# Another order and other engines for all operations of a fused attention and gated convolution kernel

## The chip, the cores and the metric

One core of a Trainium2 chip runs the whole program. The metric is device time in microseconds (us) of one launch. Five engines work side by side, each through its own list of instructions in order: TensorE (PE: matrix products, with weight loads shown as PEld), VectorE (DVE), ScalarE (ACT), GpSimd (POOL) and SyncE (SP, which issues the DMA transfers). An engine goes on only when the semaphores that its next instruction waits for have been set.

## The reference

Attention with a window and a few global keys for 4 batches x 8 heads x 768 queries x 64 elements, and then a gated convolution layer on its result. In the run `n_global` is 8 and `n_local` is 96.

```python
scores = scale * q @ k^T                      # per batch and head
is_global = pos[None, :] < n_global           # the first 8 keys
is_local = (rel >= 0) & (rel < n_local)       # the last 96 keys up to the query
dist = where(is_global & ~is_local, n_local, abs(rel))
scores = where(is_global | is_local, scores - slope[h] * dist, -1e9)
a = softmax(scores)                           # the sum gets 1e-9 added
x = a @ v                                     # heads side by side: (4, 768, 512)
gate = sigmoid(causal_conv(x, conv_w, 5 taps))    # for every channel apart
out = (gate * (x @ w_val)) @ w_out
```

The weights `w_val`, `w_out` and `conv_w` arrive as 64-bit floating point numbers, q, k and v in 32 bits; the result has 32 bits.

## The kernel before

The work is cut into 32 groups `g`: 4 batches x 2 halves of 384 queries x 4 pairs of heads. A group has three steps of 128 queries, 96 steps `s` in all. What a group goes through, with the name that the order table has for it, the line where its instruction is issued, and the engine:

- `L`, `LV`: SP loads the keys and queries `kq` and the values `va` of a group.
- `S` (line 598, PE): scores of the three steps, only for the keys that the window or the global keys can reach: at most 168 columns for each of the two heads.
- `AM` (line 606, DVE): adds the bias `bias` and takes the row minimum (`mins`) in one pass; two for each step.
- `EX` (line 616, ACT): exponential with row sum `sm`. `RG` (line 623, DVE or POOL): the guard 1e-9. `RC` (line 626, DVE): the reciprocal `rs`. `NM` (line 631, DVE or POOL): the normalisation of `p`, two for each step.
- `PT` (line 642, PE): transpositions into `pt`. `EV` (lines 298 and 300, ACT or DVE): copy of `pt` to `a`. `PV` (lines 662 and 668, PE): products with the values into `x`, for two groups together.
- `XS`, `XH`, `XL` (lines 298, 300 and 738): `x` copied to `xs` and split into a high and a low part, since an exact 32-bit product is made of three products of such parts. `CV` (lines 746 to 750): five filter taps into `gate`, the first of them on any of three engines, the others on DVE. `HI`: the four columns before a half.
- `SG` (line 779, ACT): tanh for the gate. `VM` (line 786, PE): product with `w_val`, four times four pieces of three products for each of the 8 phases (batch and half). `GM` (line 793, DVE): gate times value. `GH`, `GL` (lines 298, 300 and 800): its split.
- `OM` (line 809, PE): product with `w_out` into `o`. `OE` (lines 821 and 823): copy to `ob`. `ST` (line 828, SP): store.

Beside it run the weights, eight blocks of 128 rows or columns. `WL` loads one. `WA` (ACT) and `WZ` (line 484, POOL or DVE: the sign) read its upper halves, then DVE makes `h` (`W2`, line 494), the rounded `y` (`W3`, line 497) and the low part `r` (`W4`, line 500). `WH` copies the high part, `WS` (lines 525 to 527, PE) adds up in three products what is left into `wsum`, and `WP` copies that to the low half of the weights. `F` are filler products of PE on constants at the start (line 400), four at each of three places, and a table `FILL` names steps with further fillers before a transposition (line 637).

At the end stands a decision. If the numbers of global and local keys, or the scores, leave the range that the windows cover, a general path computes everything again after the fast one. `FA` (line 880, DVE) takes the maximum of all row minima, `FB` (line 884, PE) transposes it into `rmt`, and `FC` (lines 890 to 896, DVE) makes an integer `flag` from it in seven small instructions. Behind the last planned operation every engine reads `flag` (line 907) and branches on it (line 908). In the run the general path is not taken. The instructions of line 1119 close the program.

What sets the order: every operation is put into a plan with its kind, its engine and the operations and buffers that it needs. A table `SLOTS` has, for each kind, one number for each of its operations; the plan is sorted by it and issued in that order, and each engine receives its instructions in it. A table `ENGINES` has a letter for each operation of a kind that may run on several engines (V is DVE, S is ACT, G is POOL). Buffers are rings: an operation that reuses one waits for the readers of the old contents.

```python
e = NAMES[ENGINES[kind][n]] if kind in ENGINES else engines[0]
self.ops.append((SLOTS[kind][n], e, fn, list(deps)))
...
return [(fn, e) for _, e, fn, _ in sorted(self.ops, key=lambda op: op[0])]
...
plan.add(("FA",), (DVE,), row_mins, [("AM", s, j) for s in range(NSTEP) for j in range(2)])
plan.add(("FB",), (PE,), row_mins_t, [("FA",)] + plan.ring("pt", PT_B, ("FB",), [("FC",)]))
plan.add(("FC",), (DVE,), decide, [("FB",)])
```

Of the kernel before, what the change touches and what calls it, by code (L numbers as in the profile page):

```python
# [24 lines left out]
        2, 5, 7, 10, 30, 93, 98, 185, 233, 238, 250, 297, 338, 426, 480, 530, 594, 635, 679, 753, 845, 873, 937,  # L25
        972, 1030, 1084, 1133, 1169, 1236, 1464, 1472, 1479,
# [3 lines left out]
        19, 36, 87, 142, 191, 197, 202, 256, 275, 308, 361, 482, 485, 487, 588, 689, 718, 849, 854, 869, 1144, 1157,  # L30
        1160, 1163, 1231, 1239, 1262, 1469, 1475, 1484, 1620, 1625,
    ),
    "WARM": (0,),
    "F": (108, 27, 54),
    "IOTA": (1,),
    "UNITS": (15,),
    "CNT": (6,),
    "DIST": (9, 11),
    "BIAS": (12, 22, 13, 23, 20, 41, 18, 25, 24, 45, 26, 29, 28, 33, 37, 21),
    "WL": (4, 8, 77, 133, 175, 228, 302, 378),  # L40
    "WA": (39, 79, 139, 195, 231, 318, 394, 446),
    "WZ": (43, 106, 154, 200, 243, 328, 416, 476),
    "W2": (48, 110, 158, 211, 248, 344, 420, 483),
    "W3": (52, 117, 165, 216, 271, 354, 425, 488),
    "W4": (71, 128, 170, 220, 284, 372, 430, 497),
    "WH": (80, 127, 161, 217, 266, 355, 423, 490),
    "CWL": (14,),
    "CWA": (102,),
    "CW": (121,),
    "S": (  # L50
        17, 49, 72, 114, 166, 205, 245, 290, 333, 421, 471, 522, 587, 629, 672, 744, 796, 834, 933, 964, 1022, 1078,
        1124, 1158, 1217, 1293, 1355, 1411, 1467, 1532, 1576, 1662,
    ),
    "PV": (156, 260, 346, 453, 576, 701, 783, 922, 1007, 1142, 1250, 1341, 1453, 1567, 1699, 1751, 1778),
    "AM": (
        31, 32, 35, 38, 40, 42, 56, 58, 60, 64, 68, 69, 84, 89, 91, 94, 101, 104, 132, 135, 144, 149, 150, 160, 178,
        182, 188, 192, 194, 198, 227, 229, 232, 235, 237, 241, 257, 263, 265, 276, 278, 281, 306, 312, 316, 321,
        323, 326, 370, 377, 384, 386, 409, 414, 435, 437, 458, 461, 462, 466, 494, 495, 504, 508, 510, 513, 541,
        543, 555, 560, 573, 579, 598, 601, 605, 611, 620, 621, 638, 643, 649, 652, 654, 661, 697, 705, 712, 714,
        728, 737, 760, 767, 769, 779, 790, 793, 811, 818, 824, 826, 829, 830, 848, 863, 879, 882, 889, 891, 938,  # L60
        942, 945, 948, 950, 960, 979, 980, 993, 997, 1009, 1013, 1036, 1038, 1051, 1054, 1058, 1063, 1085, 1089,
        1096, 1102, 1116, 1118, 1135, 1136, 1141, 1145, 1147, 1154, 1170, 1178, 1185, 1198, 1200, 1206, 1225, 1232,
        1247, 1274, 1277, 1286, 1299, 1310, 1323, 1327, 1338, 1346, 1365, 1366, 1369, 1377, 1379, 1397, 1419, 1433,
        1438, 1441, 1443, 1446, 1476, 1486, 1501, 1515, 1520, 1522, 1540, 1541, 1543, 1546, 1549, 1556, 1582, 1594,
        1603, 1624, 1629, 1656, 1671, 1672, 1685, 1698, 1700, 1703,
    ),
    "EX": (
        34, 44, 47, 50, 53, 57, 61, 66, 70, 74, 85, 90, 95, 103, 109, 115, 122, 124, 136, 152, 157, 159, 164, 172,
        190, 209, 207, 212, 226, 236, 242, 246, 249, 262, 269, 289, 292, 294, 298, 307, 335, 343, 339, 349, 347,
        381, 373, 387, 397, 406, 400, 428, 419, 433, 450, 457, 481, 499, 496, 509, 518, 524, 547, 551, 561, 565,  # L70
        578, 582, 580, 583, 599, 619, 628, 631, 642, 657, 648, 650, 660, 665, 671, 677, 690, 711, 724, 729, 731,
        741, 756, 758, 765, 771, 778, 784, 809, 835, 839, 844, 855, 862, 870, 888, 892, 913, 898, 905, 908, 920,
        944, 947, 973, 1001, 975, 1004, 994, 1016, 1011, 1019, 1032, 1035, 1049, 1066, 1060, 1074, 1101, 1105, 1114,
        1120, 1122, 1128, 1125, 1149, 1139, 1151, 1184, 1203, 1191, 1207, 1199, 1248, 1224, 1243, 1230, 1237, 1265,
        1284, 1269, 1282, 1312, 1329, 1319, 1343, 1340, 1349, 1370, 1376, 1392, 1409, 1415, 1429, 1418, 1444, 1427,
        1440, 1448, 1471, 1452, 1454, 1480, 1491, 1519, 1528, 1524, 1536, 1547, 1563, 1569, 1571, 1589, 1593, 1616,
        1650, 1643, 1647, 1660, 1664, 1674, 1680, 1688, 1701, 1722, 1728,
    ),
    "RG": (
        46, 55, 76, 75, 81, 116, 123, 129, 140, 162, 167, 184, 215, 219, 244, 267, 287, 293, 301, 341, 351, 357,  # L80
        396, 402, 429, 445, 451, 464, 503, 517, 529, 564, 572, 597, 593, 627, 632, 663, 664, 670, 702, 740, 739,
        757, 780, 798, 788, 850, 876, 877, 899, 919, 924, 930, 996, 1008, 1010, 1021, 1025, 1040, 1072, 1079, 1111,
        1129, 1159, 1168, 1181, 1208, 1214, 1253, 1255, 1256, 1302, 1287, 1335, 1347, 1396, 1384, 1417, 1434, 1456,
        1455, 1478, 1489, 1497, 1533, 1564, 1575, 1584, 1610, 1661, 1665, 1705, 1708, 1737, 1730,
    ),
    "RC": (
        51, 63, 83, 88, 113, 120, 131, 145, 147, 169, 180, 189, 218, 225, 251, 270, 304, 310, 311, 350, 359, 371,
        401, 407, 434, 459, 465, 486, 506, 527, 536, 566, 596, 608, 609, 637, 641, 666, 693, 704, 707, 742, 747,
        766, 791, 800, 810, 856, 878, 903, 925, 928, 941, 946, 1012, 1015, 1020, 1041, 1046, 1070, 1087, 1095, 1127,
        1140, 1161, 1172, 1201, 1210, 1221, 1271, 1272, 1301, 1307, 1342, 1348, 1364, 1399, 1400, 1420, 1436, 1465,  # L90
        1481, 1492, 1500, 1534, 1545, 1574, 1579, 1602, 1644, 1670, 1689, 1721, 1723, 1738, 1742,
    ),
    "NM": (
        62, 59, 78, 67, 97, 99, 92, 96, 118, 125, 134, 138, 141, 148, 163, 176, 151, 181, 171, 193, 196, 186, 208,
        234, 239, 222, 230, 261, 255, 264, 280, 274, 309, 315, 327, 325, 319, 348, 362, 367, 385, 364, 375, 382,
        412, 405, 444, 441, 467, 472, 507, 470, 474, 516, 520, 519, 523, 511, 535, 563, 540, 567, 590, 577, 606,
        600, 612, 616, 634, 626, 640, 647, 659, 656, 673, 699, 713, 696, 710, 706, 719, 730, 746, 770, 763, 750,
        799, 773, 817, 814, 833, 802, 867, 838, 861, 871, 894, 881, 904, 912, 927, 935, 943, 939, 967, 970, 974,
        955, 1018, 1014, 1033, 1017, 1027, 1037, 1057, 1071, 1050, 1065, 1081, 1091, 1099, 1106, 1126, 1100, 1131,
        1138, 1153, 1174, 1164, 1173, 1188, 1183, 1215, 1216, 1242, 1219, 1228, 1222, 1275, 1280, 1295, 1279, 1305,  # L100
        1303, 1350, 1330, 1358, 1352, 1351, 1354, 1374, 1368, 1402, 1405, 1408, 1401, 1424, 1437, 1445, 1442, 1468,
        1490, 1502, 1485, 1523, 1512, 1527, 1535, 1565, 1562, 1553, 1548, 1605, 1597, 1634, 1596, 1628, 1622, 1666,
        1646, 1687, 1675, 1692, 1716, 1725, 1739, 1745, 1753, 1741, 1759, 1747, 1761,
    ),
    "PT": (
        65, 82, 105, 111, 126, 143, 153, 177, 201, 213, 214, 240, 253, 273, 282, 296, 330, 337, 358, 368, 392, 410,
        424, 448, 477, 512, 528, 544, 550, 568, 592, 603, 622, 633, 644, 655, 684, 716, 725, 751, 759, 775, 805,
        813, 822, 840, 880, 887, 900, 936, 949, 969, 989, 995, 1028, 1039, 1052, 1083, 1092, 1107, 1113, 1132, 1167,
        1179, 1196, 1209, 1223, 1261, 1267, 1297, 1304, 1311, 1361, 1372, 1380, 1393, 1423, 1430, 1447, 1474, 1506,
        1510, 1542, 1552, 1585, 1608, 1630, 1652, 1668, 1678, 1717, 1726, 1746, 1758, 1763, 1771,  # L110
    ),
    "EV": (
        73, 100, 112, 119, 137, 155, 174, 187, 206, 221, 223, 259, 272, 279, 303, 322, 334, 345, 369, 376, 408, 417,
        440, 452, 492, 526, 542, 558, 559, 574, 610, 613, 625, 639, 669, 700, 721, 738, 752, 764, 774, 781, 812,
        819, 825, 851, 885, 895, 911, 952, 968, 981, 992, 1000, 1045, 1069, 1080, 1088, 1104, 1110, 1117, 1150,
        1186, 1193, 1213, 1229, 1246, 1283, 1291, 1300, 1309, 1331, 1367, 1385, 1404, 1406, 1432, 1435, 1459, 1496,
        1509, 1517, 1560, 1566, 1609, 1614, 1651, 1655, 1677, 1682, 1724, 1729, 1749, 1764, 1769, 1774,
    ),
    "WS": (86, 130, 183, 224, 320, 379, 432, 498),
# [65 lines left out]
        1775, 1782, 1847, 1845, 1854,  # L185
    ),
    "FA": (1743,),
    "FB": (1777,),
    "FC": (1840,),
}  # L190
ENGINES = {
# [23 lines left out]
FILL = {}  # L215
# [907 lines left out]
```

## Time and profile before

| what | value |
| --- | --- |
| median of 3 runs | 267.73 us (267.15 to 268.79) |
| the profiled execution's own time | 267.06 us |
| its span in the trace | 265.3 us |
| mean granted TensorE clock | 0.998 of full speed |
| PE busy | 257.0 us, 97% |
| DVE busy | 227.5 us, 86% |
| ACT busy | 199.5 us, 75% |
| POOL busy | 96.6 us, 36% |
| HBM read and written | 29.46 MB and 6.29 MB, 135 GB/s over the span |

Times are counted from the span's start. Products of PE are pipelined, so a busy PE need not be doing its most; a product of 128x384 shows some 0.34 us and the next one starts after 0.18 us. Shares are means over stages that have different limits, so the stretches of the span are read apart. The engine names with a q at the end (PEldq, DVEq) are the parts of an engine that read registers, wait and branch.

### The profile page before, as it was taken

Reading aid. Unit: us, or ns where it says so; the run is one execution under the profiler, and the core shown is the slowest. Engines: PE = TensorE matmul, PEld = TensorE weight load, DVE = VectorE, ACT = ScalarE, POOL = GpSimd, SP = SyncE. Lnnn points to the kernel's source line nnn. Section 1 sums busy time; section 2 is a strip of 40 time slices with the busy share of each in tenths; the row PEclk is TensorE's granted clock in tenths of the full one; section 3 lists DMA queues with packets and bytes.
Section 4 is the critical chain, followed back from the end, with each engine's and each line's share of the span. In section 5 each row is a group of like instructions: output and inputs, shape, how many; then the busy total and the mean of one; then the engine's idle time right before and its main releaser. Section 6 shows DMA issues by size and latency. Waiting matters only on the chain.

```text
span 265.3 us, 8628 instructions
## 1 busy us (share of the span) xinstructions
PE 257.0 (97%) x3121; PEld 215.4 (81%) x3123; DVE 227.5 (86%) x920; ACT 199.5 (75%) x658; POOL 96.6 (36%) x211
## 2 busy tenths in 40 slices
PE   8699899999999999999999999999999999999994
PEld 3456697877899878998899878997898889878973
DVE  3998999889988999689898989799979898796930
ACT  3999999999989996977798586786978456546322
POOL 5676533462132659351131715131264410510020
PEclk9999999999999999999999999999999999999999
DMA  5996996326242730662112758100094042012003
GB/s 156 359 320 212 307 355 228 130 71 220 90 149 74 206 109 4 168 240 91 50 64 63 245 235 277 63 2 2 0 325 172 1 136 105 2 42 79 0 1 132
DMA packets 16305, 36.38 MB, mean 137 GB/s; under 512 B 1920, under 2 KB 4480, under 8 KB 16256
## 3 DMA queue, kind: packets, MB, share of 16 engines
q1 hardware_dynamic: 16256, 35.75, 40.2%
q8 instruction: 27, 0.44, 0.7%
q14 instruction: 22, 0.18, 0.2%
HBM read 29.46 MB, written 6.29 MB: 135 GB/s over the span
## 4 chain that ended last, share of the span: by engine, by line
PE 85%; DVE 6%; ACT 4%; issue 1%; DMA 1%; POOL 1%; ACTq 0%; POOLq 0%; DVEq 0%
PE o L809 25%; PE val L786 23%; PE pt L642 12%; PE s L598 9%; PE x L662 9%; PE x L668 4%; ACT p L616 2%; DVE gate L746 2%; PE wsum L525 1%; DMA counts_i<-in_counts 1%; DVE t L606 1%; POOL p L631 1%; ACT a L298 0%; DVE g L793 0%; ACT bias L464 0%
## 5 line engine op out<-in xcount | busy, mean ns | idle before, releaser
L616 ACT ACTIVATE p<-t,mins 128x168 f32<-128x168 f32 (+1 forms) x192 | 82.1, 430 | 15.5 <-PE pt L642 8.6
L631 POOL TENSOR_SCALAR p<-p,rs 128x168 f32<-128x168 f32 (+1 forms) x121 | 56.2, 475 | 82.5 <-DVE rs L626 59.8
L746 DVE SCALAR_TENSOR_TENSOR gate<-xs,cwt,gate 128x384 f32<-128x384 f32 x128 | 78.6, 631 | 0.7 <-ACT gate L748 0.4
L606 DVE CUSTOM_DVE_ANT_0 t<-s,bias 128x168 f32<-128x168 f32 (+1 forms) x192 | 55.7, 317 | 7.2 <-PE s L598 7.1
L642 PE MATMUL pt<-ident,p 128*128 128x128 f32 x272 | 47.3, 279 | 0.8 <-POOL p L631 0.5
L786 PE MATMUL val<-xh,wvh 128*128 128x384 f32 x128 | 47.5, 371 | 0.1
L786 PE MATMUL val<-xh,wvl 128*128 128x384 f32 x128 | 43.1, 337 | 0.0
L786 PE MATMUL val<-xl,wvh 128*128 128x384 f32 x128 | 43.1, 336 | 0.0
L809 PE MATMUL o<-woh,gh 128*128 128x512 f32 (+1 forms) x100 | 42.3, 423 | 0.0
L298 ACT COPY a<-pt 128x384 f32<-128x384 f32 (+1 forms) x81 | 36.3, 453 | 7.7 <-PE pt L642 7.6
L642 PEld LDWEIGHTS pt<-ident,p 128*128 128x128 f32 x272 | 33.0, 140 | 10.5 <-POOL p L631 1.6
L809 PE MATMUL o<-wol,gh 128*128 128x512 f32 (+1 forms) x100 | 38.6, 386 | 0.0
L809 PE MATMUL o<-woh,gl 128*128 128x512 f32 (+1 forms) x100 | 38.5, 385 | 0.0
L598 PEld LDWEIGHTS s<-kq 64*64 64x64 f32 x1088 | 30.1, 133 | 9.1 <-issue 5.6
L616 ACT ACTIVATION_READ_ACCUMULATOR p<-t,mins 128x1 f32 x192 | 37.3, 194 | 0.0
L598 PE MATMUL s<-kq 64*64 64x104 f32 (+3 forms) x1088 | 34.3, 262 | 2.1 <-DMA kq<-in_kq 1.7
L786 PEld LDWEIGHTS val<-xh,wvh 128*128 128x128 f32 x128 | 24.1, 188 | 0.9 <-DVE g L793 0.4
L821 ACT ACTIVATE ob<-o 128x512 f32<-128x512 f32 (+1 forms) x22 | 12.6, 577 | 16.2 <-PE o L809 16.2
L662 PE MATMUL x<-a,va 128*64 128x128 f32 x384 | 24.7, 277 | 0.0
L662 PEld LDWEIGHTS x<-a,va 128*64 128x64 f32 x384 | 20.6, 137 | 4.6 <-issue 3.8
L786 PEld LDWEIGHTS val<-xl,wvh 128*128 128x128 f32 x128 | 24.2, 189 | 0.0
L786 PEld LDWEIGHTS val<-xh,wvl 128*128 128x128 f32 x128 | 24.1, 188 | 0.0
(166 smaller groups left out, 396.6 us busy)
## 6 DMA issues: line engine op xcount, KB each, us to landing
kq<-in_kq SPq DMA_DIRECT2D x16, 444.0 KB, 4.6
va<-in_va SPq DMA_DIRECT2D x16, 384.0 KB, 6.6
out<-ob SPq DMA_DIRECT2D x24, 256.0 KB, 3.8
kq<-in_kq SPq DMA_DIRECT2D x15, 392.0 KB, 5.3
va<-in_va SPq DMA_DIRECT2D x16, 320.0 KB, 5.0
w<-in_wv SPq DMA_DIRECT2D x8, 256.0 KB, 4.5
w<-in_wo SPq DMA_DIRECT2D x3, 512.0 KB, 5.8
w<-in_wo SPq DMA_DIRECT2D x2, 256.0 KB, 3.6
```

What stands on the lines that cost most here:

```text
L298: nc.scalar.copy(dst, src)
L598: nc.tensor.matmul(s[rows, u : u + w], T["rq", g][r, k * P + half * QH : k * P + (half + 1) * QH], T["rk", g][r, c : c + w], start=True, s ...
L606: nc.vector.tensor_tensor_reduce(out=t[:, :n], in0=T["s", s // HB, s % HB, j][:, :n], in1=bias[:, h, :P] if n == P else bias[:, h, P:], op ...
L616: nc.scalar.activation(T["p", s][:, j, :n], T["t", s, j][:, :n], AF.Exp, bias=mins[:, s, j : j + 1], scale=-1.0, accum_out=T["sm", s][:, j ...
L631: engine(e).tensor_scalar(out=pr, in0=pr, scalar1=rs, scalar2=1.0, op0=ALU.mult, op1=ALU.mult)
L642: nc.tensor.transpose(pt[:, i * P : (i + 1) * P], pr[:, c : c + P], ident)
L662: nc.tensor.matmul(T["x", g][rows(i), c0 : c0 + P], T["near", g][:, k, j], T["a", HB * g + k][:, j * P : (j + 1) * P], start=k == 0, stop= ...
L668: nc.tensor.matmul(T["x", g][rows(i), c0 : c0 + QH], T["far", g][rows(j), k, h], T["a", HB * g + k][rows(j), 2 * P + h * QH : 2 * P + (h + ...
L746: nc.vector.scalar_tensor_tensor(out=gt, in0=src, scalar=w, in1=gt, op0=ALU.mult, op1=ALU.add)
L786: nc.tensor.matmul(T["val", ph, m], (wvh, wvh, wvl)[r][:, m, c * P : (c + 1) * P], (T["xh", g], T["xl", g], T["xh", g])[r], start=(c == 0 ...
L809: nc.tensor.matmul(T[key][:, cols], (T["gh", ph, c], T["gl", ph, c], T["gh", ph, c])[r][:, rows], (woh, woh, wol)[r][:, c, cols], start=(c ...
L821: nc.scalar.mul(dst, src, 0.5)
```

## The change

The two tables have other numbers and letters, and `FILL` names one step. No function is changed, and every operation of the plan is there as before. The numbers come from a longer search by annealing in which seven kinds of operations had other durations than in the search before. 45 of the 48 kinds in `SLOTS` have other numbers; a few rows are shown.

```diff
 SLOTS = {
     "L": (
-        2, 5, 7, 10, 30, 93, 98, 185, 233, 238, 250, 297, 338, 426, 480, 530, 594, 635, 679, 753, 845, 873, 937,
+        2, 5, 12, 19, 31, 92, 139, 146, 230, 316, 320, 399, 402, 412, 462, 517, 567, 734, 741, 802, 850, 991, 1016,
...
-    "F": (108, 27, 54),
+    "F": (55, 64, 28),
...
-    "FA": (1743,),
-    "FB": (1777,),
-    "FC": (1840,),
+    "FA": (1825,),
+    "FB": (1851,),
+    "FC": (1853,),
...
 ENGINES = {
-    "BIAS": "GGSSSGGGSSSSGGGV",
+    "BIAS": "SGSSSVSSVVSGGGGS",
-    "WZ": "GGGGGGGG",
+    "WZ": "GGVGGVGV",
...
     "NM": (
-        "GGVGVGGGGGGGGGVGGGGGGGVGGGGGGGGGGGVGGVVGGGGGGGGVGGGGVVVVVGVVGVVGGGGGVVGGVVGGGGGGGVGGGGGGGVGGGGGG"
-        "GGVVGGGGVVVVGGVVVVGVGVVVVGVGGGGVGGGGVVVVGGGGVVGVGVGGVGGGGVVVVGGGGGGGGVGVVVGGVVVVGGVVVVGVGVGVGVVV"
+        "VVGVGGGGVGGVGVGVVGGGVVVVVGGVVGVGVVVVVGGGVVVVGGGVGVGGGVGGVVGGGGGVVVGVVGVVGVGGGGVGVVVGVGVVVGGVVVVV"
+        "VGGVVVVGVVGVGVGGGGVVGVVGVVGVGGGGVVVVVGVVGGVVVVVVVVGVVVGVGVGVVGGVGVVVVGGVGGVVGGVGGVGVVVVVVVVVVVVV"
...
-FILL = {}
+FILL = {4: 1}
```

By the letters, the number of operations on each engine becomes: on DVE 772 instead of 712, on ACT 456 instead of 464, on POOL 143 instead of 195. Of the 192 normalisations `NM`, DVE has 112 instead of 71. SP issues the loads of the second weight block and of the taps ahead of the third `kq` instead of behind it, and the three sets of four fillers on PE stand one between the first and the second score group and two behind the second; before, one stood behind each of the first three score groups.

Three places are shown as rows of an engine's list. The names are those of the program's buffers, with their numbers; `[waits ...]` names the engines or DMA queues whose semaphore an instruction waits for.

The first is DVE around the low part of the fifth weight block, `('w', 4)_r`. Before:

```order
L497 TENSOR_SCALAR ('w', 4)_y_691<-('w', 4)_h_740 128x512
L606 ISA t_19_1_820,mins_85<-s_6_1_719,bias_78 128x168
L606 ISA mins_85 128x1
L606 ISA t_20_0_826,mins_85<-s_6_0_718,bias_78 128x168
L606 ISA mins_85 128x1
L606 ISA t_20_1_831,mins_85<-s_6_1_719,bias_78 128x168 [waits Activation_49]
L606 ISA mins_85 128x1
L500 SCALAR_TENSOR_TENSOR ('w', 4)_r_838<-w_4_560,('w', 4)_y_691 128x512 [waits DMAHW7_49,DMAHW6_49,DVE_49]
```

And in the change:

```order
L626 RECIPROCAL rs_16_822<-sm_16_783 128x2 [waits Pool_49]
L606 ISA t_20_1_825,mins_85<-s_6_1_709,bias_78 128x168
L606 ISA mins_85 128x1
L631 TENSOR_SCALAR p_14_728<-p_14_728,rs_14_806 128x168 [waits DVE_49]
L484 TENSOR_SCALAR ('w', 5)_z_835<-w_5_658 128x512 [waits DMAHW2_49]
L746 SCALAR_TENSOR_TENSOR gate_0_558<-xs0_87,cwt_84,gate_0_558 128x384
L300 CAST xh_2_862<-xs2_89 128x384 [waits Activation_49]
L631 TENSOR_SCALAR p_15_741<-p_15_741,rs_15_809 128x168 [waits DVE_49]
L738 TENSOR_TENSOR xl_2_869<-xs2_89,xh_2_862 128x384 [waits DVE_49]
L500 SCALAR_TENSOR_TENSOR ('w', 4)_r_879<-w_4_566,('w', 4)_y_694 128x512 [waits DMAHW7_49,DMAHW6_49]
```

Between the rounding of that block and its low part stood only rows of the score step; now normalisations (line 631), a sign step of the sixth block (line 484), a high part `xh` (line 300) and filter taps (line 746) stand there too.

The second is PE around the transposition `rmt`. Before, between the last product of `o` of the seventh phase's third block and the value products of group 31:

```order
L809 MATMUL o_6_2_4567<-woh_81,gl_6_3_4503 128x512
L809 MATMUL o_6_2_4567<-wol_82,gh_6_3_4467 128x512
L884 MATMUL rmt_4608<-ident_71,row_max_4519 1x128 [waits Activation_49]
L662 MATMUL x_31_4610<-a_93_4578,va_31_4227 64x128 [waits DMAHW0_49]
L662 MATMUL x_31_4610<-a_93_4578,va_31_4227 64x128
L662 MATMUL x_31_4610<-a_94_4589,va_31_4227 64x128 x2
L662 MATMUL x_31_4610<-a_95_4603,va_31_4227 64x128 [waits DVE_49]
```

In the change, the end of PE's list:

```order
L809 MATMUL o_7_2_1_4776<-woh_81,gl_7_2_4724 128x256
L809 MATMUL o_7_2_1_4776<-wol_82,gh_7_2_4711 128x256
L809 MATMUL o_7_2_1_4776<-woh_81,gh_7_3_4737 128x256
L809 MATMUL o_7_2_1_4776<-woh_81,gl_7_3_4739 128x256
L809 MATMUL o_7_2_1_4776<-wol_82,gh_7_3_4737 128x256
L884 MATMUL rmt_4791<-ident_71,row_max_4722 1x128 [waits PE_49]
L907 TENSOR_LOAD flag_86 [waits DVE_49]
L908 COMPARE_AND_BRANCH
```

The transposition, and the 104 rows of products that stood behind it have changed places: it is now PE's last instruction before the read of `flag`. Its operand `row_max` is made by `FA` on DVE.

The third is the end of DVE's list. Before:

```order
L793 SCALAR_TENSOR_TENSOR g_7_2_4716<-gate_7_4473,val_7_2_4681 128x384 [waits PE_49,Activation_49]
L793 SCALAR_TENSOR_TENSOR g_7_3_4728<-gate_7_4473,val_7_3_4691 128x384 [waits PE_49,Activation_49]
L823 TENSOR_SCALAR ob_7_0_4755<-o_7_0_4724 128x512 [waits DMAHW4_49,DMAHW5_49,DMAHW3_49,DMAHW7_49,DMAHW2_49,PE_49]
L890 TENSOR_REDUCE far_4760<-rmt_4608 1x1
L891 TENSOR_SCALAR slow_4761<-counts_70 1x1
L892 SCALAR_TENSOR_TENSOR slow_4761<-counts_70,slow_4761 1x1 [waits DVE_49]
L893 SCALAR_TENSOR_TENSOR slow_4761<-counts_70,slow_4761 1x1 [waits DVE_49]
L894 SCALAR_TENSOR_TENSOR slow_4761<-far_4760,slow_4761 1x1 [waits DVE_49]
L895 TENSOR_SCALAR slow_4761<-slow_4761 1x1 [waits DVE_49]
L896 CAST flag_86<-slow_4761 1x1 [waits DVE_49]
L907 TENSOR_LOAD flag_86 [waits DVE_49]
```

In the change:

```order
L800 TENSOR_TENSOR gl_7_2_4724<-g_7_2_4703,gh_7_2_4711 128x384 [waits DVE_49]
L793 SCALAR_TENSOR_TENSOR g_7_3_4732<-gate_7_4425,val_7_3_4699 128x384 [waits PE_49,Activation_49]
L300 CAST gh_7_3_4737<-g_7_3_4732 128x384 [waits DVE_49]
L890 TENSOR_REDUCE far_4794<-rmt_4791 1x1 [waits PE_49]
L891 TENSOR_SCALAR slow_4795<-counts_70 1x1
L892 SCALAR_TENSOR_TENSOR slow_4795<-counts_70,slow_4795 1x1 [waits DVE_49]
L893 SCALAR_TENSOR_TENSOR slow_4795<-counts_70,slow_4795 1x1 [waits DVE_49]
L894 SCALAR_TENSOR_TENSOR slow_4795<-far_4794,slow_4795 1x1 [waits DVE_49]
L895 TENSOR_SCALAR slow_4795<-slow_4795 1x1 [waits DVE_49]
L896 CAST flag_86<-slow_4795 1x1 [waits DVE_49]
L907 TENSOR_LOAD flag_86 [waits DVE_49]
```

The seven small instructions still close DVE's list. What they wait for on PE is now the transposition at PE's end; before, it was one that stands far ahead in PE's list, and a copy of an output block `ob` stood in front of them.

## Rows read from the trace of the kernel before

**Rows 1.** The page, busy time of each engine, and granted clock in 40 slices.

```profile
PE 257.0 (97%) x3121; PEld 215.4 (81%) x3123; DVE 227.5 (86%) x920; ACT 199.5 (75%) x658; POOL 96.6 (36%) x211
...
PEclk9999999999999999999999999999999999999999
```

**Rows 2.** Busy time by stretch: length, PE, PEld, DVE, ACT, POOL, clock, DMA, GB/s.

```profile
5.30:32.70 27.40, 23.81 (x356) 16.39 (x354) 25.13 (x133) 26.69 (x101) 17.34 (x45) 1.00 0.88 298
32.70:43.40 10.70, 10.70 (x163) 8.96 (x161) 10.58 (x46) 10.48 (x34) 4.46 (x11) 1.00 0.89 331
43.40:248.90 205.50, 205.50 (x2528) 178.02 (x2528) 184.35 (x723) 157.60 (x517) 70.21 (x140) 1.00 0.34 113
248.90:261.40 12.50, 12.42 (x69) 10.51 (x67) 5.96 (x17) 3.06 (x6) 1.99 (x2) 1.00 0.10 36
261.40:265.30 3.90, 0.00 (x1) 0.00 (x0) 0.00 (x0) 0.39 (x1) 0.00 (x0) 0.89 0.32 112
```

**Rows 3.** Timeline of DVE: start, duration, engine, line, operation, out and in.

```profile
46.29 0.67 DVE L500 SCALAR_TENSOR_TENSOR ('w', 5)_r<-w,('w', 5)_y 128x512 fp32r<-128x512 uint32 x1
46.88 0.28 DVE L606 CUSTOM_DVE_ANT_0 t<-s,bias 128x128 f32<-128x128 f32 x1
```

**Rows 4.** Timeline of PE, 46.5 to 49.8 us.

```profile
46.88 0.42 PE L786 MATMUL val<-xh,wvh 128*128 128x384 f32 x1
...
47.49 1.02 PE L525 MATMUL wsum<-('w', 5)_h,ident 128*128 128x512 f32 x2
...
48.58 0.39 PE L527 MATMUL wsum<-('w', 5)_r,units 128*128 128x512 f32 x1
```

**Rows 5.** Line 631 on DVE: duration in ns, least, median and most.

```profile
L631 DVE TENSOR_SCALAR p<-p,rs x71: 268/303/1065, 12.6 to 237.3; 128x168 f32<-128x168 f32 x65, 128x128 f32<-128x128 f32 x6
```

**Rows 6.** Waits of DVE, 0 to 45 us: in total, times, longest.

```profile
DVE ('w', 2)_h L494 <- POOL ('w', 2)_z L484: 0.8, 1, 0.8
DVE ('w', 1)_h L494 <- POOL ('w', 1)_z L484: 0.4, 1, 0.4
```

**Rows 7.** Groups of DVE, 3 to 52 us: busy us, mean ns, idle before.

```profile
L623 DVE TENSOR_SCALAR sm<-sm 128x2 f32<-128x2 f32 x19 | 3.7, 198 | 0.7 <-ACT p L616 0.4
...
L631 DVE TENSOR_SCALAR p<-p,rs 128x168 f32<-128x168 f32 x7 | 2.5, 356 | 0.0
...
L750 DVE TENSOR_SCALAR gate<-xs,cwt 128x384 f32<-128x384 f32 x1 | 0.9, 902 | 0.0
```

**Rows 8.** Line 884, the transposition `rmt`: ns least, median, most; first and last start.

```profile
L884 PE MATMUL rmt<-ident,row_max x1: 272/272/272, 242.0 to 242.0; 128*1 128x128 f32 x1
```

**Rows 9.** Timeline of DVE, 257 to 266 us: the seven small instructions, first and last.

```profile
257.85 0.27 DVE L890 TENSOR_REDUCE far<-rmt 1x1 f32<-1x128 f32 x1
...
258.93 0.14 DVE L896 CAST flag<-slow 1x1 int32<-1x1 f32 x1
```

**Rows 10.** Timeline of all engines, 260.3 to 265.3 us: the last product and copy.

```profile
261.12 0.28 PE L809 MATMUL o<-wol,gh 128*128 128x256 f32 x1
261.44 0.39 ACT L821 ACTIVATE ob<-o 128x256 f32<-128x256 f32 x1 [0.66 <-PE o L809]
```

**Rows 11.** Line 907, the read of `flag`.

```profile
L907 DVEq TENSOR_LOAD <-flag x1: 546/546/546, 259.1 to 259.1; - x1
```

**Rows 12.** Line 908, the branch and the semaphores behind it.

```profile
L908 DVEq COMPARE_BRANCH  x1: 72/72/72, 259.7 to 259.7; - x1
L908 PEldq COMPARE_BRANCH  x1: 3807/3807/3807, 260.0 to 260.0; - x1
...
L908 ACTq COMPARE_BRANCH  x1: 50/50/50, 262.0 to 262.0; - x1
...
L908 ACTq EVENT_SEMAPHORE  x1: 17/17/17, 262.4 to 262.4; - x1
L908 DVEq EVENT_SEMAPHORE  x1: 21/21/21, 262.8 to 262.8; - x1
```

**Rows 13.** Line 1119, the closing join.

```profile
L1119 SPq DRAIN  x3: 7/7/13, 264.5 to 264.8; - x3
```

## Prediction before the run

> **What bounds the kernel now.** I read the page's first part, then the stretches, then the waits of the vector engine, then single rows at the two places where the change does most. TensorE (PE) is busy for 97% of the span, at the full clock throughout [rows 1]. The stretches say what that share is made of: from 32.7 to 248.9 us PE is busy for every microsecond of every stretch, while the vector engine (DVE) still has some 21 us free in the longest one, and before 32.7 us PE is idle for 3.6 of 27.4 us although ScalarE (ACT) and DVE are nearly full [rows 2]. So there are three parts. In the head, DVE and ACT decide when PE gets its work. In the middle PE goes from product to product, and only the amount of its work counts. Behind the last product come 3.9 us of copying, storing and ending [rows 2]. An order can gain only where PE idles, and lose wherever it makes PE wait.
>
> **PE's own work.** Both orders hold the same 386 groups on PE. Changes between products on the whole array and products on 64-wide tiles number 78 in either order, and one filler product more stands in the head, where PE idles anyway; with that cover gone it would be one product of the length of its neighbours, under half a microsecond. The steady part therefore costs what it did: 0.
>
> **The head.** The change takes 41 normalisations from GpSimd (POOL) and gives them to DVE, and 60 operations more in all; many of these stand early. The place where that is dearest is the sixth weight block. Its low part `('w', 5)_r` is computed by DVE at 46.29 us and ends at 46.96 [rows 3]; PE's third product of `wsum` reads it at 48.58 [rows 4]. So there are 1.6 us to spare. In the new order 28 instructions more of DVE stand ahead of it (223 instead of 195, counted one by one): 14 normalisations, 8 rows of the score step, 3 filter taps, two sign steps and, after others cancel, one more. DVE handles one instruction in 0.19 us between 5.3 and 32.7 us (25.13 us for 133) and in 0.23 us after that (10.58 for 46) [rows 2]: 5.3 to 6.4 us. A normalisation is 0.303 us in the median [rows 5] and overlaps its successor by 0.08, as the low part does, 0.67 long but followed after 0.59 [rows 3]; I take 5.6. PE has one group of value products more to do before that place, 0.6 us (46.88 to 47.49) [rows 4]. 5.6 - 1.6 - 0.6 = 3.4 us late, if DVE waits and is slowed as now. From this comes off what DVE can win back. It waited 0.8 and 0.4 us for sign steps on POOL [rows 6], which the new order either lists earlier there or does on DVE itself; and some of its early instructions ran long beside POOL: 0.356 for a normalisation instead of 0.303, 0.902 for the first tap, 0.198 for a guard [rows 7], together about 2 us before 52 us. All of it recovered leaves 0.2 us. ACT gives a second reading: 7 instructions more stand ahead of the last copy that the third `x` product needs (99 operations instead of 92), at 0.28 us on the mean of 135 in 37.2 us [rows 2] that is 1.9 us, against about 1.2 us more of PE's work there: 0.7 us late. Between 0.2 and 3.4 I take **+1.3**, nearer to ACT's value, since a part of DVE's early waits should go. Moved loads: the third `kq` is now issued behind the second weight block and the taps, 532 KB that take 1.8 us at 298 GB/s [rows 2]; DVE has work listed there, so I charge nothing beyond the range above. The fillers, now eight behind the second score group, lie under the same cover.
>
> The trace shows DVE's normalisation at 0.303 us in the median and 1.065 at most [rows 5], the long ones beside POOL. [...]
>
> **The end.** The decision between the fast path and the general one is made from `rmt`, a transposition on PE, then seven small DVE instructions, then a read of `flag` by every engine and a branch. Now the transposition stands at 242.0 us [rows 8] and the flag is ready at 259.07 [rows 9], before PE ends at 261.40 [rows 10]. The new order puts it behind the last product, and the seven behind that. From PE's end: about 0.1 us for the transposition (0.27 long, overlapping; bounds 0 and 0.27), 1.22 for the seven (257.85 to 259.07) [rows 9], then DVE's read of the flag, and from its start at 259.1 [rows 11] to DVE's last semaphore at 262.8 [rows 12] 3.7 us, most of it behind a branch that itself takes 0.07. The closing join starts at 264.5 [rows 13] and the span ends 0.8 later. 0.1 + 1.2 + 3.7 + 0.8 and 0.2 for three handovers make 6.0 us after PE's end, where now there are 3.9 [rows 2]: **+2.1**. The last store, landed by 264.5, no longer decides. PE's own branch takes 3.8 us [rows 12]; were none of that its wait for its products (1.4 us, 260.0 to 261.4), PE would come last, and it would be +2.7. The lower bound is ACT, 0.45 us from branch to semaphore [rows 12]: with that the flag ends before the store lands, +0.
>
> The branch rows of DVE and PE lie at 3 us and more to the next event [rows 12]. [...]
>
> **Sum.** 267.06 (the profiled execution: 265.3 of span and what lies around it) + 1.3 + 2.1 = 270.5. That execution lies 0.67 below the median of the runs shown, 267.73, so the median to expect is **271.1 us**, 1.3% slower.
>
> **Rivals.** (a) The branch is cheap where the target is near, and the store still comes last: then only the head counts, 267.7 + 1.3 = 269.0. For it speaks ACT's row, against it DVE's and PE's. 12%. [...] (b) DVE recovers its early waits and PE reaches its full stretch as early as now: only the end counts, 269.8. For it: 1.2 us of waits that have a named cause. 20%. (c) DVE becomes the bound beyond the head. Fourteen microseconds of work go to it (227.5 [rows 1] to about 241), between 3.5 us and about 252 us. If a third of the 21 us that it now idles in the middle stays as waits for inputs, the 7.5 us left are used up and some 4.5 us reach PE, with the end: 274.3. For it: DVE is already at 10.58 of 10.70 where the head ends [rows 2]. Against it: most of that idle time is idle because DVE is ahead. 13%. (d) The other side, faster: PE's 3.6 idle us of the head [rows 2] are filled, because sign steps and first normalisations come without waiting on POOL. It beats 1% only if nearly all of it, 3.0 us, is won and the end stays hidden as in (a): 264.7. It decides at PE starting its first full stretch before 30 us. 5%. My forecast has the other 50%, its own range 269.4 to 273.0.
>
> **How the numbers follow.** About 1%, 2.7 us, is what a measurement here can tell from no change. Slower by more: (c), seven tenths of the forecast and a little of (b), 0.52. Faster: (d), 0.05. The rest, 0.43. The range goes from 268.0, which takes in (b) and most of (a), to 274.0, which takes in half of (c) and both ends of the costs.
>
> **What would show it.** The transposition `rmt` as PE's last product, `flag` written after PE's end, and DVE's or PE's last semaphore more than 4.5 us after it would show the end. The third `wsum` product of weight 5 waiting for DVE, or PE's last idle time lying after 33 us, would show the head. Wrong I would be if the span ended 4 us after PE's last product, if PE ended before 261 us, or if PE had idle time between 60 and 240 us, which is (c).

## The result and the profile after

The change takes 271.63 us (median of 6 runs, 271.26 to 272.67) where the kernel before takes 267.62 beside it: ratio 1.0137, interval 1.011 to 1.0165, 4.0 us. The forecast was 271.1. The profiled execution took 272.67 us, 1.0 above the median, with a span of 270.8. The page first (busy time, and granted clock in 40 slices), which answers to [rows 1]:

```profile
PE 258.3 (95%) x3124; PEld 216.8 (80%) x3124; DVE 236.0 (87%) x980; ACT 194.6 (72%) x650; POOL 72.6 (27%) x159
...
PEclk9799999999999999999999999999999999999996
```

PE did the same work, 1.4 us longer by this count, in a span that is 5.5 us longer. The busy time by stretch (columns as in [rows 2]; the last two boundaries are PE's end and the span's):

```profile
5.30:32.70 27.40, 23.69 (x309) 15.11 (x309) 24.92 (x137) 25.41 (x92) 10.91 (x25) 0.94 0.83 280
...
43.40:248.90 205.50, 204.76 (x2551) 177.87 (x2550) 190.53 (x768) 152.54 (x510) 56.51 (x111) 1.00 0.36 121
248.90:263.90 15.00, 14.99 (x87) 13.59 (x85) 7.37 (x17) 3.85 (x9) 1.02 (x1) 1.00 0.19 69
263.90:270.80 6.90, 0.00 (x0) 0.00 (x0) 1.06 (x7) 0.30 (x1) 0.00 (x0) 0.70 0.15 52
```

Four things differ from [rows 2]. The head ran at a mean granted clock of 0.94 instead of 1.00, by a stretch at the lower level that the last section shows; kernel 10, whose head is the same and whose clock did not fall, has its first transposition 1.3 us earlier, so about 1.3 us of this execution lie there. PE ends at 263.9 instead of 261.4. Behind it stand 6.9 us instead of 3.9, with seven instructions of DVE in them. And PE idles 0.74 us in the long middle, where it idled not at all. The last product of `o` ends 0.11 us before the transposition does, at 263.79, so what lies behind the products is 7.0 us. The chain at the end, in answers on lines 884, 908 and 1119 (ns least, median, most; first and last start) and a timeline of DVE, with line 828 for the last store:

```profile
L884 PE MATMUL rmt<-ident,row_max x1: 270/270/270, 263.6 to 263.6; 128*1 128x128 f32 x1
```

```profile
263.93 0.28 DVE L890 TENSOR_REDUCE far<-rmt 1x1 f32<-1x128 f32 x1 [6.78 <-PE rmt L884]
...
265.02 0.14 DVE L896 CAST flag<-slow 1x1 int32<-1x1 f32 x1
```

```profile
L908 DVEq COMPARE_BRANCH  x1: 72/72/72, 265.9 to 265.9; - x1
L908 PEldq COMPARE_BRANCH  x1: 3827/3827/3827, 265.9 to 265.9; - x1
...
L908 DVEq EVENT_SEMAPHORE  x1: 21/21/21, 269.0 to 269.0; - x1
L908 PEldq EVENT_SEMAPHORE  x1: 51/51/51, 269.8 to 269.8; - x1
```

```profile
L1119 SPq DRAIN  x3: 7/7/13, 270.0 to 270.3; - x3
...
L1119 DVEq EVENT_SEMAPHORE  x2: 21/21/21, 270.2 to 270.7; - x2
```

```profile
L828 SPq DMA_DIRECT2D out<-ob x1: 332/332/332, 264.2 to 264.2; - x1
...
DMA to landing us min/median/max: 2.0/2.0/2.0
```

Read them as one path: transposition, 1.2 us of small instructions, 0.6 for the read on line 907 (595 ns on DVE), 3.83 for PE's branch, 1.0 to close. The last store has landed by 266.2, and the closing join starts at 270.0, 0.2 behind PE's semaphore. Every engine reads at 265.2, since all wait for the flag; in [rows 12] PE's branch began at 260.0, under its own last products.

### The profile page after: what moved, and what is told of

The parts are those of the page before. It is cut to its first block, busy times and chain, and to the rows that moved or that the text cites. A ratio compares the mean times of both kernels' runs of the same rounds, so it can differ in the third digit from the quotient of the medians.

```text
span 270.8 us, 8618 instructions
## 1 busy us (share of the span) xinstructions
PE 258.3 (95%) x3124; PEld 216.8 (80%) x3124; DVE 236.0 (87%) x980; ACT 194.6 (72%) x650; POOL 72.6 (27%) x159
## 4 chain that ended last, share of the span: by engine, by line
PE 87%; DVE 5%; ACT 2%; DMA 2%; SPq 1%; issue 1%
PE o L809 25%; PE val L786 23%; PE pt L642 12%; PE s L598 10%; PE x L662 8%; PE x L668 4%; PE wsum L525 2%; DMA kq<-in_kq 2%; DVE t L606 1%; PE warm L400 1%; DVE gate L746 1%; ACT p L616 1%; PE wsum L526 1%; PE wsum L527 1%; DVE gl L800 0%
## 5 line engine op out<-in xcount | busy, mean ns | idle before, releaser
L631 POOL TENSOR_SCALAR p<-p,rs 128x168 f32<-128x168 f32 (+1 forms) x80 | 37.7, 480 | 72.2 <-DVE rs L626 55.3
L642 PE MATMUL pt<-ident,p 128*128 128x128 f32 x272 | 46.4, 281 | 0.8 <-ACT wvl L298 0.3
L298 ACT COPY a<-pt 128x384 f32<-128x384 f32 (+1 forms) x83 | 37.8, 457 | 12.5 <-PE pt L642 12.4
L786 PE MATMUL val<-xh,wvh 128*128 128x384 f32 x128 | 46.5, 363 | 0.0
L809 PE MATMUL o<-woh,gh 128*128 128x512 f32 (+1 forms) x100 | 41.1, 411 | 0.0
L642 PEld LDWEIGHTS pt<-ident,p 128*128 128x128 f32 x272 | 32.3, 141 | 9.2 <-ACT a L298 1.2
L616 ACT ACTIVATION_READ_ACCUMULATOR p<-t,mins 128x1 f32 x192 | 38.0, 198 | 0.0
L631 DVE TENSOR_SCALAR p<-p,rs 128x168 f32<-128x168 f32 (+1 forms) x112 | 32.4, 300 | 0.2
L623 POOL TENSOR_SCALAR sm<-sm 128x2 f32<-128x2 f32 x28 | 9.7, 348 | 54.4 <-ACT p L616 33.2
```

The source lines that it names most:

```text
L298: nc.scalar.copy(dst, src)
L616: nc.scalar.activation(T["p", s][:, j, :n], T["t", s, j][:, :n], AF.Exp, bias=mins[:, s, j : j + 1], scale=-1.0, accum_out=T["sm", s][:, j ...
L631: engine(e).tensor_scalar(out=pr, in0=pr, scalar1=rs, scalar2=1.0, op0=ALU.mult, op1=ALU.mult)
L642: nc.tensor.transpose(pt[:, i * P : (i + 1) * P], pr[:, c : c + P], ident)
L786: nc.tensor.matmul(T["val", ph, m], (wvh, wvh, wvl)[r][:, m, c * P : (c + 1) * P], (T["xh", g], T["xl", g], T["xh", g])[r], start=(c == 0 ...
L809: nc.tensor.matmul(T[key][:, cols], (T["gh", ph, c], T["gl", ph, c], T["gh", ph, c])[r][:, rows], (woh, woh, wol)[r][:, c, cols], start=(c ...
```

## The experiments

Each kernel was timed beside the kernel before; its ratio to that is given with the interval. Kernel 1 is that of experiment 1, and so on. "PE's last product" is the end of the last product of `o` in the trace: 261.40 us before, 263.79 in the change.

**1. The change with the decision early.** The numbers with .5 lie between two others.

```diff
-    "FA": (1825,),  "FB": (1851,),  "FC": (1853,),
+    "FA": (1724.5,), "FB": (1760.5,), "FC": (1832.5,),
```

> The change with one thing put back: the row maximum right after the last score step, its transposition ahead of the value products of group 31, the seven small instructions behind the last low part on DVE. Head and middle stay those of the change. Theory (the decision behind the last product costs the end): after the last product 3.9 us remain as before, instead of 7.0, so 271.6 - 3.1 = 268.5 us. Rival (PE's branch begins only once PE has finished its products, wherever the flag is made): only the transposition and the seven instructions come off, 1.4 us, 270.2 us. Second rival (the end is not what changed, the whole loss lies in the head): 271.6 us.

269.33 us, ratio 1.0055 (1.003 to 1.008): 2.3 us of the 4.0 come off by the medians, between theory and first rival. The span ends 4.2 us after PE's last product (262.18 to 266.4). The branches, the closing join and the last store:

```profile
L908 DVEq COMPARE_BRANCH  x1: 72/72/72, 258.1 to 258.1; - x1
...
L908 PEldq COMPARE_BRANCH  x1: 4082/4082/4082, 260.8 to 260.8; - x1
...
L908 PEldq EVENT_SEMAPHORE  x1: 51/51/51, 264.9 to 264.9; - x1
```

```profile
L1119 SPq DRAIN  x3: 7/7/13, 265.5 to 265.9; - x3
```

```profile
L828 SPq DMA_DIRECT2D out<-ob x1: 332/332/332, 262.6 to 262.6; - x1
...
DMA to landing us min/median/max: 2.8/2.8/2.8
```

With the flag made early DVE jumps at 258.1, long before the end, and PE's branch starts 1.4 us before its last product ends. The rival that it waits for PE's products falls. Of the branches PE's still ends last, 2.7 us behind that product, but the join starts only at 265.5, when the last store has landed: issued at 262.6, it takes 2.8 us. It is this store, 0.3 slower than in the kernel before, that makes 4.2 us out of 3.9. In the traces it takes 2.6 to 3.2 us where an engine jumps over the general path while it is under way (the kernel before and kernels 1, 5 to 8 and 10), and 2.0 where it has all but landed when the jump begins, or where there is none (the change and kernels 2, 3, 4 and 9). Under this store three packets of instructions move in the kernel before (261.8 to 264.4 us) and none in the change (264.2 to 266.2). That such packets hold it up is a guess; no kernel tries that alone.

**2. The kernel before with the decision late.**

```diff
-    "FB": (1777,),  "FC": (1840,),
+    "FB": (1852.5,), "FC": (1853.5,),
```

> The kernel before with the same thing put in: the transposition as PE's last operation and the seven small instructions as DVE's last. Theory: 267.6 + 3.1 = 270.7 us, with PE's last product where it was (261.4 us) and 7 us behind it. Rival (branch waits for PE's products anyway): 269.0 us. If the end alone made the change slower, this kernel would take 271.6 us.

271.27 us, ratio 1.0132 (1.0103 to 1.0162): 3.5 us from this alone, nearly the change's whole loss. PE's last product ends at 262.51, since this execution has a wait of 1.1 us that the profile calls "issue"; the span ends 7.4 us later, PE's branch taking 4.2:

```profile
L908 PEldq COMPARE_BRANCH  x1: 4207/4207/4207, 264.6 to 264.6; - x1
```

**3. The head of the kernel before.** A program joins the two orders: operations whose old number is at most 529 keep number and engine, the others get 10000 plus the new number, and the new engine.

```diff
-    SLOTS[kind][n] = new[kind][n]
+    SLOTS[kind][n] = old[kind][n] if old[kind][n] <= 529 else 10000 + new[kind][n]
```

> The first 530 operations in the order and on the engines of the kernel before (to about 67 us), everything behind them in the order of the change, decision late. Theory (DVE and ACT in the new head make PE late by about 2 us): PE's last product comes 2 us earlier than in the change, 269.6 us. Rival (the head's loss in the profiled execution is only the stretch at the lower clock, 10.9 to 14 us, that other executions need not have): 271.0 to 271.6 us. Rival (c) of the prediction (DVE is the bound later on and takes back what the head gives): 271.6 us.

271.77 us, ratio 1.0163 (1.013 to 1.0196): no gain, a miss. PE's last product ends at 262.06, 1.7 us earlier than in the change, close to the theory; but the change's profiled execution also had the stretch at the lower clock, and kernel 1, which has the change's head without that stretch, ends its last product at 262.18, only 0.1 later. And the end takes 8.7 us. PE's branch is 4.45 us here, and then DVE is late in the closing join (line 1119, as above):

```profile
L1119 PEldq EVENT_SEMAPHORE  x2: 51/51/51, 269.1 to 270.8; - x2
L1119 DVEq EVENT_SEMAPHORE  x2: 21/21/21, 270.5 to 270.8; - x2
```

PE signals at 269.1, DVE 1.4 us later; in the change both did at 270.2. The seam also cost PE 1.2 us near 70 us: the product in front of the score group there starts at 69.14 us, where kernel 1 starts it at 70.31, and behind that group both are level (71.68). So the head of before was 1.2 us ahead, and lost it at the seam. The median can't show it; kernel 10 is the cleaner test.

**4. The change without the general path.** It leaves that path out, with one small instruction in its place; the run does not take it.

```diff
     with tc.If(slow):
-        general(tc, const, ident, counts, (wvh, wvl, woh, wol), cwt, qT, kg, v, out)
+        nc.vector.memset(cwt[:, 0, :], 0.0)
```

> The change, but the general path behind the branch is left out and one small instruction stands in its place. Theory (what DVE and PE lose behind the branch goes with the length of the code that they jump over; ACT and POOL, which take 0.45 us and less, jump over little): DVE's and PE's last semaphores come within 0.6 us of the branch instead of 3.1 and 3.9, the span ends some 3 us earlier, 268.6 us. Rival (a branch after a flag costs PE and DVE this much whatever stands behind it): 271.6 us.

268.58 us, ratio 1.0028 (0.9995 to 1.006): 3.1 us less than the change, as the theory said. Line 908, and then what the DMA queues carried (packets, MB, share) from the branch to the end, in the change (265.9 to 270.8 us) and here (264.9 to 266.7):

```profile
L908 PEldq COMPARE_BRANCH  x1: 220/220/220, 265.0 to 265.0; - x1
L908 DVEq EVENT_SEMAPHORE  x1: 21/21/21, 265.1 to 265.1; - x1
```

```profile
q8 instruction: 2, 0.03, 3.1%
q14 instruction: 4, 0.03, 2.0%
```

```profile
q1 hardware_dynamic: 1, 0.00, 0.0%
```

The same branch takes 0.22 us instead of 3.83, and the span ends 3.9 us after PE's last product (262.83 to 266.7), as in the kernel before, though the flag is late. In the change six packets of instructions move behind the branch, here none. So the price, 3.1 us by the medians, belongs to the code that is jumped over, not to branch, flag or read. By the program's text the path left out holds some 340 operations of PE and 280 of DVE, but 13 of ACT and 7 of POOL, whose semaphores came 0.5 us or less behind their branches in the change too. Whether PE's 3.83 us are a wait for those packets is not shown.

**5. DVE relieved in the head.** Decision early, as in 1; the first 48 normalisations on the engines of before.

```diff
-    "NM": after[:48] + ...,
+    "NM": before[:48] + ...,
```

> The change with the early decision, and the first 48 normalisations on the engines of the kernel before (8 on DVE instead of 26; POOL has the others). Order unchanged. Theory (the 0.7 us that PE still loses more than before between 26 and 50 us are ACT's: the third weight sum waits for a copy of `a`, and ACT has seven more operations ahead of it): DVE's relief gives nothing, 269.3 us, the wait for the copy stays 0.5 us. Rival (the prediction's place: DVE's 14 more normalisations make PE late): 0.7 us come off, 268.6 us. Third: POOL takes 0.41 us for a normalisation where DVE takes 0.30, and PE waits for it: slower than 269.3 by 0.5 or more.

269.73 us, ratio 1.0067 (1.004 to 1.0094): no gain. The waits of PE from 14 to 60 us (us in total, times, longest):

```profile
PE pt L642 <- POOL p L631: 1.0, 1, 1.0
...
PE wsum L525 <- ACT a L298: 0.6, 1, 0.6
PE pt L642 <- ACT a L298: 0.4, 1, 0.4
```

The waits for ACT stay, and one for a normalisation on POOL is new. From the low part of the third weight block to that of the fourth, where kernel 10 below finds PE falling behind, PE takes 5.56 us (26.46 to 32.02), as in kernel 1 (5.55). DVE's added normalisations were not what made PE late there.

**6. ACT relieved in the head.** Decision early; two first taps and a history copy go from ACT to POOL.

```diff
-    "CV"[0], "CV"[5], "HI"[0]: "S"
+    "CV"[0], "CV"[5], "HI"[0]: "G"
```

> The change with the early decision, and three of ACT's operations of the head on POOL, which idles there: the first filter taps of groups 0 and 1 (0.62 us each on ACT, 0.6 to 0.96 on POOL) and the first four-column history (0.19). Order unchanged. Theory (ACT makes PE late in the new head): ACT reaches the copy that the fourth weight block's sum waits for about 1.2 us earlier, PE's waits between 26 and 50 us fall by 0.5 to 0.8 us, 268.6 us. Rival (DVE is the bound there): PE's waits stay, 269.3 us. [...]

269.79 us, ratio 1.0062 (1.0035 to 1.0088): no gain, 0.5 above kernel 1 by the medians, with intervals that overlap. PE's longest wait in the same stretch, and POOL's tap in the timeline:

```profile
PE pt L642 <- DVE sm L623: 1.2, 1, 1.2
```

```profile
29.49 0.98 POOL L750 TENSOR_SCALAR gate<-xs,cwt 128x384 f32<-128x384 f32 x1 [0.66 <-ACT xs L298]
...
30.02 0.73 DVE L497 TENSOR_SCALAR ('w', 3)_y<-('w', 3)_h 128x512 int32<-128x512 int32 x1
```

The waits for a copy of `a` are gone, as expected, but one for DVE takes their place, and PE takes 5.76 us between the two low parts instead of 5.55. Beside POOL's tap DVE's rounding took 0.73 us, where it took 0.41 to 0.43 in the kernel before; that could make 0.3 of the wait of 1.2, the rest has no cause shown. This execution is 1.5 us above its kernel's median and has a granted clock of 0.61 from 11 to 14 us, so its later waits may differ from those of the others. By the names of its waits PE is held up by ACT in this order, but taking three operations from ACT gained nothing.

**7. One low part on DVE.** Decision early.

```diff
-    "GL"[18]: "G"
+    "GL"[18]: "V"
```

> The change with the early decision, and one low part (line 800, phase 4, block 2) on DVE instead of POOL. In the traces of this order DVE's low part of block 0 runs at the same time as this one and takes 1.39 us instead of 0.55, and PE then waits for the low part of block 1 and starts the second product of `o` 0.5 us late. Theory (two engines hold each other up at the same kind of instruction): DVE's low part takes 0.55 us again, PE's 0.5 us are gone, 268.8 us. Rival (DVE is simply behind there, its queue decides): the wait moves to another product and the time stays at 269.3 us.

268.61 us, ratio 1.0039 (1.0015 to 1.0063), 0.7 below kernel 1 by the medians, though the intervals overlap. The timelines of kernel 1 and of this one:

```profile
178.78 1.02 POOL L800 TENSOR_TENSOR gl<-g,gh 128x384 fp32r<-128x384 f32 x1 [7.34 <-ACT gh L298]
178.81 1.39 DVE L800 TENSOR_TENSOR gl<-g,gh 128x384 fp32r<-128x384 f32 x1
...
180.26 0.50 PE L809 MATMUL o<-woh,gl 128*128 128x512 f32 x1 [0.27 <-DVE gl L800]
```

```profile
178.81 0.56 DVE L800 TENSOR_TENSOR gl<-g,gh 128x384 fp32r<-128x384 f32 x1
179.35 0.56 DVE L800 TENSOR_TENSOR gl<-g,gh 128x384 fp32r<-128x384 f32 x1
...
179.84 0.39 PE L809 MATMUL o<-woh,gl 128*128 128x512 f32 x1
```

Started 0.03 us after POOL's, DVE's low part takes 1.39 us; alone it takes 0.56, PE's wait is gone and the products behind it start 0.5 us earlier. Part of that is lost again: at 228.7 us three transpositions take 0.77 us instead of 0.49, and PE's last product ends at 261.98, 0.2 before that of kernel 1. DVE's part takes 0.83 us more beside POOL's of 1.02; by what means the two hold each other up is not shown.

**8. Two orders joined.** Kernel before up to number 1499, the change behind it, decision early.

```diff
-    SLOTS[kind][n] = new[kind][n]
+    SLOTS[kind][n] = old[kind][n] if old[kind][n] <= 1499 else 10000 + new_early[kind][n]
```

> The order and engines of the kernel before for its first 1500 operations (to about 195 us), the change's for the rest, decision early. Theory: head and middle cost what they did, the change's last phase has none of the 0.7 us for which PE waited for DVE from 247 to 252 us, and the end is that of before: 267.7 - 0.7 = 267.0 us. Rival (the seam costs PE a wait, as at 70 us in the kernel with the head of before): 267.7 to 268.5 us.

267.13 us, ratio 0.9981 (0.9964 to 0.9999): 0.6 below the kernel before by the medians, as the theory had it, with an interval that ends just under 1. The traces show half of it: PE is 0.58 us later than in the kernel before at the low part of the sixth weight block (49.16 and 48.58) and 0.27 later at the end of its last product (261.67 and 261.40), so the change's last phase gives 0.3 back, though not by named waits.

**9. The joined order without the general path**, left out by the edit of experiment 4.

> The joined order with the early decision, and the general path left out (one small instruction in its place). In the joined order PE's branch begins at 260.3, takes 4.5 us and ends at 265.0, while the last store was issued at 262.1 and such a store lands 2 us later, at about 264.1. Theory (the early decision hides the branch only in part: PE's branch and the store end within a us of each other): the branch gone, the store decides, some 0.9 us come off, 266.2 us. Rival (the store hides the branch fully): 267.1 us. Rival (all that lies behind PE's last product is branch): 2 us off, 265.1 us.

266.7 us, ratio 0.9962 (0.9938 to 0.9985); 0.4 less than kernel 8 by the medians. PE's branch in kernel 8 and here:

```profile
L908 PEldq COMPARE_BRANCH  x1: 4545/4545/4545, 260.3 to 260.3; - x1
```

```profile
L908 PEldq COMPARE_BRANCH  x1: 220/220/220, 259.7 to 259.7; - x1
```

Here PE's branch is over at 259.9, 1.1 us before PE's last product ends, so it did not wait for products. In the traces the time from that product to the end falls from 4.3 us (261.67 to 266.0) to 3.4 (261.01 to 264.4), the 0.9 of the theory; the medians show half of it. The theory had the store landing at 264.1 in kernel 8. It landed at 264.9, together with the end of PE's branch, 2.8 us after its issue; here it takes 2.0. An early decision hides most of the jump, not all: what is left is as much the store's delay as PE's.

**10. The head of the change, then the kernel before.**

```diff
-    SLOTS[kind][n] = old[kind][n]
+    SLOTS[kind][n] = new[kind][n] if new[kind][n] <= 529 else 10000 + old[kind][n]
```

> The first 530 operations in the order and on the engines of the change (to about 70 us), everything behind them as in the kernel before, decision early as there. Theory (the new head by itself costs 0.7 us, of which PE's waits for copies by ACT between 26 and 50 us are 1.0 and the earlier waits give 0.4 back): 267.7 + 0.7 = 268.4 us, a little more if the seam makes PE wait. Rival (the prediction's middle value, 1.3): 269.0 us. Rival (the head costs nothing, what the early-decision kernel has above the kernel before comes from the middle): 267.7 us.

268.67 us, ratio 1.0041 (1.0025 to 1.0057): 1.1 us, between theory and the rival of 1.3. The low parts of the third and fourth weight blocks on PE, in the kernel before and here:

```profile
25.62 0.39 PE L527 MATMUL wsum<-('w', 2)_r,units 128*128 128x512 f32 x1
...
30.31 0.40 PE L527 MATMUL wsum<-('w', 3)_r,units 128*128 128x512 f32 x1
```

```profile
25.62 0.39 PE L527 MATMUL wsum<-('w', 2)_r,units 128*128 128x512 f32 x1
...
31.18 0.39 PE L527 MATMUL wsum<-('w', 3)_r,units 128*128 128x512 f32 x1
```

Level at the third, PE is 0.9 us late at the fourth, and 1.4 at its last product (262.85 and 261.40), whose order is that of the kernel before. PE's waits from 24 to 60 us here:

```profile
PE wsum L525 <- ACT a L298: 0.7, 2, 0.5
PE pt L642 <- ACT a L298: 0.3, 1, 0.3
PE pt L642 <- DVE sm L623: 0.2, 1, 0.2
```

and in the kernel before:

```profile
PE wsum L525 <- ACT a L298: 0.5, 1, 0.5
PE pt L642 <- ACT wvl L298: 0.2, 1, 0.2
```

1.2 us instead of 0.7, the larger part for ACT. So named waits make 0.5 of the 1.1 to 1.4; what makes the rest is open.

## Why the prediction was right, term by term

**Bounds.** The reading by three parts held. What an order gains or loses stands in the head, in single waits of the middle, and behind the last product.

**The end, +2.1.** The mechanism was right: the transposition is PE's last instruction, the flag is made behind it, and the branch is then on the path. The term was too small. It measured 3.1 in the profiled execution (7.0 instead of 3.9), 3.5 in kernel 2 and 2.3 in kernel 1. The step that failed is the choice of DVE as the engine that ends last: the prediction left open whether PE's 3.8 us in [rows 12] were in part a wait for its products, and kept PE for its upper bound. They were no wait: 3.83 us with every product done, and 0.22 with products still running in kernel 9. So PE's semaphore came at 269.8, 0.8 behind DVE's. The upper bound, +2.7, was the right case, and the join adds some tenths more. Kernel 4 shows that the price is that of the jump, which the prediction saw as rows only.

**The head, +1.3.** The size was near: 1.1 by the medians of kernel 10 and 1.4 in its trace, seam included. The place was wrong. The prediction worked it out at the low part of the sixth weight block on DVE; that is now made later, but in time (DVE and PE of the change):

```profile
50.48 0.68 DVE L500 SCALAR_TENSOR_TENSOR ('w', 5)_r<-w,('w', 5)_y 128x512 fp32r<-128x512 uint32 x1
```

```profile
51.62 0.39 PE L527 MATMUL wsum<-('w', 5)_r,units 128*128 128x512 f32 x1
```

It ends 0.46 us before PE reads it, where [rows 3, 4] had 1.6. PE falls behind earlier, ahead of the fourth weight block's low part. DVE won early waits back, as the low end assumed: a normalisation is 0.304 us in the mean there, not the 0.356 of [rows 7]. The "about 2 us" for instructions that ran long is more than its rows give, some 1.5: 0.4 for the normalisations, 0.5 for the tap against the median first tap on DVE (0.42), 0.6 for the guards against their mean in the change (0.164). The second reading, by ACT's seven more operations, named the engine that PE's waits name, and gave 0.7; those waits grow by 0.5.

**The middle, 0.** Wrong by parts that nearly cancel. Two low parts that met on POOL and DVE cost 0.5 at their place (kernel 7), the new last phase gives 0.3 back in the traces (kernel 8), and the profiled execution has 0.5 of a wait without a named releaser in the scores of group 24, which kernels 1 and 7, with the same order there, lack. From PE's waits in the change, 60 to 262 us:

```profile
PE s L598 <- issue: 0.5, 1, 0.5
```

An order's middle does count, then: it decides which instructions of POOL and DVE meet.

**Rivals.** (a) falls with kernels 2 and 4: PE's branch is cheap where the target is near, 0.22 us in kernel 4, but here it is not near, and takes 3.8 to 4.5. (b) falls with kernel 10. Of (c) one sign was there, PE idle for 0.74 us between 150 and 200 us, but for other reasons than DVE's load: DVE's busy time grew by 8.5 us (227.5 to 236.0), not by 14. Its price of 4.5 us does not come out of its own numbers either, since 7.5 us left less a third of 21 leaves 0.5 free. (d) did not happen.

The pieces, 1.1 for the head, 0.5 - 0.3 for the middle and 3.1 for the end, make 4.4 for the 4.0 measured, where the prediction had 3.4. Executions of one kernel scatter by a microsecond and more, so this is agreement and no proof of each, and that the forecast came within 0.5 us with an end 1.0 too small is in part luck.

## What to carry to other kernels

A branch over long code cost 3 to 4.5 us here on the two engines with the most code behind it, however small the branch itself reads (0.07 us on DVE), and packets of instructions moved meanwhile, six in the change. Make the flag early enough that PE's jump begins under its last products, or shorten the code that is jumped over, and look at the last store, which took 2.6 to 3.2 us instead of 2.0 beside a jump; a search that prices the decision as seven small instructions has no reason not to put it last. When an engine gets more work, look first at how much of its old time was lost to waits and to running beside another engine (1.39 us instead of 0.56 for a low part here), and at the engine that has no slack at all.

## What the runs showed that was not expected

In the head PE's second score group waits for its keys, and that differs between executions of the same head: kernels 2, 8 and 9 issue the same head, and PE waits there for 1.2, 2.3 and 1.2 us and starts that group at 8.56, 9.72 and 8.71 us. Some 0.65 us of the difference is left at the third score group (11.74, 12.39 and 11.72).

In the change's profiled execution the granted clock was 0.50 of full speed from 11 to 14 us, after PE had idled from 7.5 to 9.2 us; in kernel 10, with the same head, it stayed at 1.00 from 5.3 to 32.7. The eight fillers stand there (PE's timelines of the two):

```profile
10.34 3.29 PE L400 MATMUL warm<-const-bfloat16-1.0 128*128 128x512 bf16 x8
```

```profile
10.36 1.92 PE L400 MATMUL warm<-const-bfloat16-1.0 128*128 128x512 bf16 x8
```

They took 1.4 us longer at the lower level, and the first transposition came 1.3 us later. In kernel 6's trace the clock fell at the same place. Why it fell in these two and not in the others is open: in kernel 10 PE had idled a little longer than in the change, from 7.4 to 9.3 us.

The same closing code costs more or less from kernel to kernel: PE's branch took 3.8 to 4.5 us over the same path, and in kernel 3 DVE's join came 1.4 us behind PE's. What decides this is open.
